# Causal scores packed in 64-key halves: 18 score units a segment in place of 20, with a padded copy of V and a new timetable

## The chip, the cores and the metric

The kernel runs on one core of one Trainium2 chip. The metric is the device time of one execution in microseconds (us). Engines: PE (TensorE), ACT (ScalarE), DVE (VectorE), POOL (GpSimd), SP (SyncE, which here only issues DMAs).

## The reference

The input x has 2048 tokens of 640 features. It is normalized per token, and two blocks read the result xn: block A, attention with 32 heads of 20 features in 4 segments of 512 tokens with a running memory, and block B, a gated MLP of width 1536.

```python
xn = _layernorm(x)
# block A, for each of the 4 segments s (L = 512), all 32 heads:
logits = einsum('bhqd,bhkd->bhqk', qs, ks) * 20**-0.5 + causal_mask
a_dot = einsum('bhqk,bhkd->bhqd', softmax(logits), vs)
a_mem = einsum(phi(qs), M) / (einsum(phi(qs), z) + 1e-6)   # M, z: sums over earlier segments
o = g * a_mem + (1 - g) * a_dot                            # g = sigmoid(beta), per head
M = M + einsum(phi(ks), vs); z = z + sum(phi(ks))
s = o @ wo
# block B and the end
h = (sigmoid(xn @ w_gate) * (xn @ w_up)) @ w_down
out = x + s * silu(h)
```

The mask is causal inside a segment: a query sees the keys up to its own place. phi(t) is t + 1 where t > 0, else exp(t).

## The kernel before

**Scores and attention.** The 32 heads are 8 groups g of 4 heads r. Queries and keys are kept transposed (QT, KT): head r of a group has its 20 features and 3 rows of a softmax bound in partitions 32r to 32r+22, so that the four heads' score matmuls (23 rows by 128 keys) run in four row groups of PE. Their products go to the four PSUM banks of Sps, head r to bank r, keys on the partitions, queries along the bank. One filling of Sps (512 columns in each bank) is a score unit: scores (L544) computes it, exps (L552) makes one exponential of 128x2048 on ACT into a tile pt (4 buffers), and POOL masks the 128 columns at the diagonal of each key block with affine_select (L557).

Of key block kb (128 keys) the queries from 128 kb on are computed: 512, 384, 256 and 128 columns, 1280 a group. pair_units (L44) packs two groups in five units of 512 columns, so a segment has 20 units and the kernel 80.

attend_T (L561) multiplies a group's pt tiles by V. V (Vflat, two buffers, one for each parity of the segment) has tokens on its partitions and for each key block and head 20 features and a column of ones. For each of the four key blocks it issues four matmuls, one per head, side by side in four column groups of 32, all into the bank ApsT: 16 matmuls. Three steps in "turn" (L578 to L594) transpose the result on DVE, divide it (on POOL mostly) and transpose it back. The last group of the last segment goes through attend (L598) and finalize instead, with queries on the output's partitions: 40 matmuls of 21 columns.

**Dense work.** Gate, up and down projections are generators that give one matmul a step (do_gate, do_up, do_down). mm (L117) issues a matmul whole, or as four in column groups of 32 while ORDER["columns"] is set; that is so in a slot that is followed by an attend. PSUM has 4 banks for Sps and 4 (pool ps_d, L96) for all else.

**The order** is written out by hand. Each score unit opens a slot. A slot does the attend that is due in it (visits), then scores and exps of its unit, then events, sorted by their times in the table TIMES (in slots from the segment's start), with dense steps in between so that the work done keeps up with a constant rate per slot (L922 to L948). Events are the projections K, Q and V of the next segment with their evacuations (K_eng, Q_eng, V_eng: a for ACT, v for DVE), layer norm, phi, the memory's parts, spills of Q and K to DRAM and their read-back in the head layout (spill, relayout), the spill of the attention's output (dot_spill) and its read-back in another layout (out_load), and the output projection. After the last unit, the remaining down projections and the output of the last segment follow (tail_*). All DMAs after the start-up are issued by SP in order, except two of the last stores; each waits there until its data are ready.

At the start PE runs a warm-up on a zeroed tile (keep_warm_columns, L636, called at L642), and segment 0 is normalized and projected in straight order (L643 to L754).

Of the kernel before, what the change touches and what calls it, by code (L numbers as in the profile page):

```python
# [43 lines left out]
def pair_units(g):  # L44
    return [[(g, 0, 0, 512, 0)],
            [(g, 1, 0, 384, 128), (g, 3, 384, 128, 384)],
            [(g, 2, 0, 256, 256), (g + 1, 2, 256, 256, 256)],
            [(g + 1, 0, 0, 512, 0)],
            [(g + 1, 1, 0, 384, 128), (g + 1, 3, 384, 128, 384)]]

def segment_units(n):
    units = []
    for g in range(0, NG, 2):
        units += pair_units(g)
    return units

TIMES = dict(
    turn=(0.03, 0.27, 1.29), turn_last=(0.0, 0.135, 0.43), attend=0.36, last=(0.36, 0.75), rest=350, dot6=0.43, load6=0.48,
    dot7=1.92, load7=1.95, add=(4.27, 4.52), out=(5.25, 5.95, 7.25, 8.35, 8.74, 9.06, 9.45, 11.05), update=-1.2,
    mem=(2.23, 4.32, 3.0, 6.98, 6.98, 2.45, 9.09, 10.79), mem_spill=11.56, mem_T=14.4, mem_T_last=12.63,  # L60
    k_tok=2.04, dot3=13.22, dot5=17.84, load5=18.1, add5=19.86, dot6_last=19.55, load6_last=19.6, stats0=(0.53, 0.9, 1.65, 3.6),
    stats=(-0.55, 0.13, 1.32, 3.57), norm=(5.26, 5.72, 6.03, 6.29), norm_T=7.22, ready=12.0,
    K=(9.69, 10.07, 10.49, 13.82, 14.29), Q=(11.32, 11.72, 12.29, 12.45, 13.52), K_eng='vaava', Q_eng='avvav',
    V=(10.33, 13.33, 14.43, 14.63, 17.05, 17.66, 19.78, 20.06), V_eng='avaavvav', k_spill0=14.77, k_lay0=15.15,
    q_spill0=14.1, q_lay0=16.79, q_spill1=15.26, k_spill1=16.93, q_abs=(13.53, 14.84), bound=14.78,
    bound_mm=15.9, bound_lay0=18.6, load_x=13.95, phi_k=((7.15, 7.62, 8.3), (12.77, 13.52, 13.77)),
    phi_q=((16.0, 16.6, 17.12), (18.3, 18.7, 19.18)),
# [8 lines left out]
def kernel(  # L76
# [37 lines left out]

    xt_of, xnT_of = {}, {}
# [29 lines left out]
    warm = stg.tile([P, 3 * L], BF, name="mn")  # L145
    nc.vector.memset(warm[:, 0:L], 0.0)
# [33 lines left out]
    V = [t[:, 0:VN].rearrange("p (j h e) -> p j h e", j=4, e=E1) for t in Vflat]  # L180

# [56 lines left out]
    def ln_norm(n, j, mv, rs):  # L238
        if n > 0 and j < 2:
            if j == 0:  # L240
                seg["xn"] = stg.tile([P, 3 * L], BF, name="mn")
            xn = seg["xn"][:, j * D:(j + 1) * D]
        else:
            xn = lnp.tile([P, D], BF, name="xn", bufs=2)[:]
# [81 lines left out]
    def bound_mm(n):  # L326
# [6 lines left out]
        cb = stg.tile([3 * H, L], BF, name="cb")  # L333
# [23 lines left out]
    def phi_min(n, key, c0, c1):  # L357
        src = seg[n][key][:, c0:c1, :]
        mn = stg.tile([P, 3 * L], BF, name="mn")
# [17 lines left out]
    def m_update(n):  # L377
# [13 lines left out]
        dmb = stg.tile([P, DC, WIN], BF, name="dmb")  # L391
# [111 lines left out]
    HALF = P // 2  # L503
    o6 = cpool.tile([HALF, L], BF, name="o6")
    nc.gpsimd.memset(o6[:].bitcast(mybir.dt.uint32), 0)

    def tail_load():
        src = OTd[(NSEG - 1) % 2]
        nc.sync.dma_start(seg[NSEG - 1]["oT"][R5 - C3:P, 3, :], src[R5:C4, :])
        nc.sync.dma_start(o6[0:R6 - C4, :], src[C4:R6, :])  # L510
# [10 lines left out]
    def tail_add4(j0, j1):  # L521
        t = slice(j0 * P, j1 * P)
        nc.vector.tensor_tensor(seg[NSEG - 1]["oT"][0:HALF, DC - 1, t],
                                tail_po[j0][:].rearrange("p j t -> p (j t)")[0:HALF, :], o6[:, t], op=ALU.add)
# [18 lines left out]

    def scores(unit):  # L544
        for (g, kb, c0, ncol, q0) in unit:
            for r in range(4):
                nc.tensor.matmul(Sps[:, r, c0:c0 + ncol],  # L547
                                 lhsT=KT[32 * r:32 * r + DH + 3, g, kb * P:(kb + 1) * P],
                                 rhs=QT[32 * r:32 * r + DH + 3, g, q0:L],
                                 start=True, stop=True, tile_position=(32 * r, 0))  # L550

    def exps(unit):  # L552
        ntot = sum(u[3] for u in unit)
        pt = ptp.tile([P, 4, L], BF, name="pt")
        nc.scalar.activation(pt[:, :, 0:ntot], Sps[:, :, 0:ntot], ACT.Exp, scale=SCALE)  # L555
        for (g, kb, c0, ncol, q0) in unit:
            nc.gpsimd.affine_select(out=pt[:, :, c0:c0 + P], in_=pt[:, :, c0:c0 + P], compare_op=ALU.is_ge,  # L557
                                    fill=0.0, base=0, pattern=[[0, 4], [1, P]], channel_multiplier=-1)
        return pt

    def attend_T(n, g, todo):  # L561
# [6 lines left out]
        for i, ((_, kb, c0, ncol, q0), t) in enumerate(todo):  # L568
            for r in range(4):
                off = (kb * H + 4 * g + r) * E1  # L570
                nc.tensor.matmul(ps[32 * r:32 * r + 32, q0:L], lhsT=Vflat[n % 2][:, off:off + 32],  # L571
                                 rhs=t[:, r, c0:c0 + ncol], start=(i == 0), stop=(i == len(todo) - 1),
# [25 lines left out]
    def attend(n, todo):  # L598

        if not acc:  # L600
            acc["ps"] = ps_d.tile([P, 4, 4, E1], F32, name="Aps", tag="d")
            acc["blocks"] = 0
        for (g, kb, c0, ncol, q0), t in todo:
            for r in range(4):
                for qb in range(kb, 4):
                    off = c0 + (qb - kb) * P
                    nc.tensor.matmul(acc["ps"][:, qb, r, :], lhsT=t[:, r, off:off + P],
                                     rhs=V[n % 2][:, kb, 4 * g + r, :],
                                     start=(acc["blocks"] == 0 and r == 0 and qb == kb), stop=True,
                                     skip_group_check=True)  # L610
            acc["blocks"] += 1
        if acc["blocks"] == 4:
# [29 lines left out]
    keep_warm_columns(17, L // 2)  # L642
# [17 lines left out]
    def norm0(j, *pieces):  # L660
        nc.vector.reciprocal(rs[:, j:j + 1], rs[:, j:j + 1])
        xns[j] = lnp.tile([P, D], BF, name="xn", bufs=2)
# [79 lines left out]
    bound_dma(0, 0)  # L742
    load_x(1)
# [31 lines left out]
    units = [(n, unit) for n in range(NSEG) for unit in segment_units(n)]  # L775
    units.append((NSEG - 1, None))
    SLOTS, SEG = len(units), 20
    LAST = (NSEG - 1) * SEG
    OLD = LAST + 15
# [7 lines left out]
    for p in range(0, OLD, 5):  # L787
        n, g = units[p][0], units[p][1][0][0]
        visits[p + 4] = (n, g, (p, p + 1, p + 2))
        visits[p + 6] = (n, g + 1, (p + 3, p + 2, p + 4))  # L790
    visits[OLD + 4] = (NSEG - 1, NG - 2, (OLD, OLD + 1, OLD + 2))

# [9 lines left out]
    for slot, (n, g, _) in visits.items():  # L802
        for k in range(3):
            late = g == NG - 1 or slot == OLD + 4
            at(slot + TIMES["turn_last" if late else "turn"][k], 0, turn, n, g, k)

    def last_attend(slots):
        todo = [(p, pts[u]) for u in slots for p in units[u][1] if p[0] == NG - 1]
        attend(NSEG - 1, todo)

    for slot in range(OLD + 1, OLD + 4):
        at(slot + TIMES["attend"], RESERVE, lambda: None)
    at(OLD + 4 + TIMES["last"][0], 500, last_attend, (OLD + 2, OLD + 3))
    at(OLD + 5 + TIMES["last"][1], 500, last_attend, (OLD + 4,))

# [13 lines left out]
    for n in range(NSEG):  # L829
# [7 lines left out]
        if n >= 1:  # L837
# [14 lines left out]
        if n == NSEG - 1:  # L852
            on("dot5", 0, dot_spill, (n, 4, 6))
# [68 lines left out]
    for slot, (n, unit) in enumerate(units):  # L922
        if slot in visits:
            m, g, us = visits[slot]
            attend_T(m, g, [(q, pts[u]) for u in us for q in units[u][1] if q[0] == g])
# [79 lines left out]
```

## Time and profile before

| | |
|---|---|
| three runs, us | 316.82, 316.96 (median), 317.26 |
| the profiled execution, us | 316.93 |
| its span, first to last instruction, us | 315.2 |
| first and last score unit start, us | 35.52 and 296.88 |
| last matmul starts, us | 311.2 |
| ACT: 80 exponentials, us each | 1.878 |
| POOL: 128 masks of 128x512, us each | 0.658 |
| DVE / POOL busy | 72% / 42% |
| DMA, mean | 131 GB/s |

Times inside the span count from its start. An engine's share is busy time over the span; it is an average over stages. In a list of groups, a line gives the source line, engine, operation, tiles, shapes, count, then busy us and mean ns of one, then the engine's idle time just before such instructions and what ended it. The chain that ended last follows the end of the program back to what released each step. L numbers are lines of the kernel before.

### The profile page before, as it was taken

To read this page: it belongs to the slowest core of one execution; us is meant where nothing else is said; L and a number is where in the kernel's file an instruction comes from. 1 tells how busy PE (TensorE), PEld (TensorE's weight loads), DVE (VectorE), ACT (ScalarE), POOL (GpSimd) and SP (SyncE) were. 2 spreads that over 40 slices of the span, in tenths; PEclk is the share of its full clock that TensorE was granted. 3 is DMA by queue.
4 is the path that set the end of the run, shared out by engine and by line. 5 is a ranking of instruction groups with operands and counts; after the bars stand their busy time and mean duration, and the time that the engine had idled before them with its cause. 6 is when DMAs were issued, how large, how long until landed. Compare 5 with 4: busy or idle time off the path is not lost.

```text
span 315.2 us, 10264 instructions
## 1 busy us (share of the span) xinstructions
PE 309.9 (98%) x4329; PEld 167.5 (53%) x4329; DVE 225.7 (72%) x512; ACT 226.8 (72%) x231; POOL 131.6 (42%) x227
## 2 busy tenths in 40 slices
PE   7999999999999999999999999999999999999995
PEld 5544445665545445654665454544466655444673
DVE  6574455665868988878879989788777776644575
ACT  3723478778798776778897869679897775777730
POOL 2680035535262435435453354444434353525313
PEclk9999999999999999999999999999999999999999
DMA  8984886510841364405954445139534000280202
GB/s 250 361 340 144 282 228 163 153 32 2 217 146 65 101 131 148 107 23 150 247 170 123 115 108 152 61 111 215 163 91 125 19 23 30 79 156 16 86 21 85
DMA packets 55247, 41.27 MB, mean 131 GB/s; under 512 B 25953, under 2 KB 53825, under 8 KB 55201
## 3 DMA queue, kind: packets, MB, share of 16 engines
q1 hardware_dynamic: 52656, 35.87, 41.0%
q10 hardware_dynamic: 2544, 4.75, 4.0%
q8 instruction: 34, 0.56, 0.7%
q14 instruction: 13, 0.10, 0.1%
HBM read 19.98 MB, written 14.73 MB: 110 GB/s over the span
## 4 chain that ended last, share of the span: by engine, by line
PE 96%; DVE 2%; DMA 1%; issue 0%
PE up L121 12%; PE yp L121 11%; PE gp L121 11%; PE psq L121 10%; PE Sps L547 8%; PE gp L125 6%; PE yp L125 6%; PE up L125 6%; PE ApsT L571 6%; PE psv L121 5%; PE psq L125 4%; PE sp L121 3%; PE sp L125 3%; PE psv L125 2%; PE sp L531 2%; PE am L121 1%
## 5 line engine op out<-in xcount | busy, mean ns | idle before, releaser
L555 ACT ACTIVATE pt<-Sps 128x2048 bf16<-128x2048 f32 x80 | 150.2, 1878 | 40.9 <-PE Sps L547 39.6
L557 POOL TENSOR_SCALAR_AFFINE_SELECT pt<-pt 128x512 bf16<-128x512 bf16 x128 | 82.2, 658 | 156.2 <-ACT pt L555 153.4
L434 DVE SCALAR_TENSOR_TENSOR hT<-tg,up 128x512 bf16<-128x512 bf16 x48 | 32.5, 678 | 24.0 <-PE up L121 9.7
L121 PE MATMUL up<-xnT,Wu 128*128 128x512 bf16 x159 | 42.5, 380 | 0.0
L121 PE MATMUL gp<-xnT,Wg 128*128 128x512 bf16 x152 | 40.1, 380 | 0.0
L423 ACT ACTIVATE tg<-gp 128x512 bf16<-128x512 f32 x48 | 28.5, 595 | 14.4 <-PE gp L121 10.5
L121 PE MATMUL yp<-Wd,hT 128*128 128x320 bf16 x246 | 38.2, 300 | 0.0
L547 PE MATMUL Sps<-QT,KT 23*128 23x384 bf16 (+3 forms) x512 | 31.9, 301 | 0.0
L121 PEld LDWEIGHTS <-hT 128*128 128x128 bf16 x246 | 22.7, 98 | 11.3 <-issue 3.0
L579 DVE STREAM_TRANSPOSE tb<-ApsT 128x512 f32<-128x512 f32 x31 | 22.0, 711 | 4.2 <-PE ApsT L571 4.0
L451 DVE SCALAR_TENSOR_TENSOR aa<-t,yp 128x320 bf16<-128x320 bf16 x32 | 15.3, 477 | 12.9 <-ACT t L450 12.7
L125 PE MATMUL gp<-xnT,Wg 128*32 128x512 bf16 x352 | 24.4, 380 | 0.0
L571 PE MATMUL ApsT<-pt,V 128*32 128x512 bf16 (+2 forms) x496 | 23.5, 299 | 0.0
L121 PEld LDWEIGHTS <-Wu 128*128 128x128 bf16 x159 | 14.2, 98 | 17.4 <-issue 4.0
L121 PEld LDWEIGHTS <-Wg 128*128 128x128 bf16 x152 | 14.1, 98 | 15.8 <-issue 1.9
L125 PE MATMUL yp<-Wd,hT 128*32 128x320 bf16 x552 | 21.9, 300 | 0.0
L125 PE MATMUL up<-xnT,Wu 128*32 128x512 bf16 x324 | 21.7, 380 | 0.0
L547 PEld LDWEIGHTS <-KT 23*128 23x128 bf16 x512 | 9.1, 92 | 23.4 <-issue 23.4
L591 DVE STREAM_TRANSPOSE obT<-ob 128x256 f32<-128x256 f32 x31 | 13.4, 434 | 11.1 <-POOL ob L588 11.0
L588 POOL TENSOR_TENSOR ob<-tb,rb 128x320 bf16<-128x320 f32 x27 | 19.8, 735 | 2.2
L121 PE MATMUL psq<-xnT,Wq 128*128 128x512 bf16 x85 | 19.5, 379 | 0.0
L571 PEld LDWEIGHTS <-V 128*32 128x32 bf16 x496 | 14.4, 97 | 8.1 <-ACT tg L423 0.2
(124 smaller groups left out, 447.3 us busy)
## 6 DMA issues: line engine op xcount, KB each, us to landing
KT<-Kd SPq DMA_DIRECT2D x32, 80.0 KB
QT<-Qd SPq DMA_DIRECT2D x32, 80.0 KB
out_dram<-xt SPq DMA_DIRECT2D x14, 160.0 KB
Wg<-in_B_w_gate_dram ACTq DMA_DIRECT2D x1, 1920.0 KB
Wu<-in_B_w_up_dram ACTq DMA_DIRECT2D x1, 1920.0 KB
xt<-in_A_x_dram SPq DMA_DIRECT2D x3, 640.0 KB
Wd<-in_B_w_down_dram SPq DMA_DIRECT2D x1, 1920.0 KB
Od<-odot SPq DMA_DIRECT2D x3, 640.0 KB
```

The costliest lines, as they stand in the source:

```text
L121: nc.tensor.matmul(out_, lhsT=lhsT, rhs=rhs, start=start, stop=stop, skip_group_check=True)
L125: nc.tensor.matmul(out_[cols], lhsT=lhsT[:, cols], rhs=rhs, start=start, stop=stop, tile_position=(0, 32 * r), skip_group_check=True)
L423: nc.scalar.activation(tg[:], gp[:], ACT.Tanh, scale=0.5)
L434: nc.vector.scalar_tensor_tensor(out=h[:], in0=seg[n]["tg"][:], scalar=1.0, in1=up[:], op0=ALU.add, op1=ALU.mult)
L451: nc.vector.scalar_tensor_tensor(out=s["aa"][j][:, hs], in0=t2[:], scalar=1.0, in1=yp[:], op0=ALU.add, op1=ALU.mult)
L547: nc.tensor.matmul(Sps[:, r, c0:c0 + ncol], lhsT=KT[32 * r:32 * r + DH + 3, g, kb * P:(kb + 1) * P], rhs=QT[32 * r:32 * r + DH + 3, g, q0: ...
L555: nc.scalar.activation(pt[:, :, 0:ntot], Sps[:, :, 0:ntot], ACT.Exp, scale=SCALE)
L557: nc.gpsimd.affine_select(out=pt[:, :, c0:c0 + P], in_=pt[:, :, c0:c0 + P], compare_op=ALU.is_ge, fill=0.0, base=0, pattern=[[0, 4], [1, P ...
L571: nc.tensor.matmul(ps[32 * r:32 * r + 32, q0:L], lhsT=Vflat[n % 2][:, off:off + 32], rhs=t[:, r, c0:c0 + ncol], start=(i == 0), stop=(i == ...
L579: nc.vector.transpose(tb[:].rearrange("p h e -> p (h e)"), ps[:].rearrange("p (a t b) -> p a b t", t=32, b=2))
L588: eng.tensor_tensor(to, of, by, op=ALU.mult)
L591: nc.vector.transpose(s["obT", g // 4][:, g % 4, :].bitcast(F32), ob[:].rearrange("p a e b -> p (a e b)").bitcast(F32))
```

## The change

The causal triangle is cut finer, in blocks of 64 keys, and the pieces are packed anew. The units of four groups (e to e+3) are nine, in the order A, B, Y, A, W, A, Y, A, B; a segment has 18 and the kernel 72. All are full, 512 columns in each bank.

- A: key block 0. Keys 0-63 give partitions 0-63 and queries 0-511; keys 64-127 give partitions 64-127 and queries 64-511. The 64 columns left over in the upper half take keys 128-191 with queries 128-191.
- B: key block 1 from query 192, and key block 2 from query 320, both with all 128 keys.
- W: key block 2 from query 320 and key block 3 from query 448, for two groups, all 128 keys.
- Y: key block 1 from query 192 (two halves of 64 keys), key block 3 from query 448 of a group (two halves), and the two 64x64 triangles at keys 256 and 384 for two groups, one in each half.

A and Y issue their matmuls with 64 keys (23 rows by 64 columns of the array); A has 12 matmuls, B 8, W 16 and Y 32. The number of score matmuls goes from 512 to 1152.

The 64x64 triangles at queries 0, 128, 256 and 384 need V of 64 keys only; for them there is a padded copy Z, whose other 64 partitions are zero. Z holds the 16 heads of half a segment. fill_Z copies V into it with two DMAs on SP, once in the start-up and then twice a segment (slots 1.97 and 10.49). An attend has 8 pieces in place of 4, five of 64 columns, 32 matmuls. attend for the last group cuts queries in 64: 80 matmuls.

POOL masks 64 columns per diagonal block: A takes two affine_selects, B two, W two, Y four.

All times of the table are new. Seven of eight V evacuations per segment are on ACT (four before), four of five of K (three before), and two of Q as before. The read-back of the first 512 rows of a segment's attention output (load6) is at 0.58 of the next segment, the fill of Z at 1.97, and the spill and read-back of the rest (dot7, load7) at 2.29 and 2.54. Small tiles share a buffer (tag sc: xn of the fourth token block, cb, dmb, o6), xn of the first three is in mn, and the warm-up has 38 rounds of 112 columns in place of 17 of 256.

```diff
+    for e in range(0, NG, GH):
+        units += [("A", e), ("B", e), ("Y", e + 1), ("A", e + 1), ("W", e + 1),
+                  ("A", e + 2), ("Y", e + 2), ("A", e + 3), ("B", e + 3)]
...
+    ZW = H // 2 * E1
+    Zflat = cpool.tile([P, 4 * ZW + 32 - E1], BF, name="Z")
+    Z = Zflat[:, 0:4 * ZW].rearrange("p (a b w) -> p a b w", a=2, b=2)
+
+    def fill_Z(n, h):
+        src = Vflat[n % 2][0:HALF, 0:VN].rearrange("p (a b k w) -> p a b k w", a=2, b=2, k=2)
+        for b in range(2):
+            nc.sync.dma_start(Z[HALF * b:HALF * b + HALF, :, b, :], src[:, :, b, h, :])
...
+        nc.gpsimd.memset(Zflat[:], 0.0)
...
+    def products(pieces):
+        for out_, keys, g, q0, q1 in pieces:
+            m, p0 = keys.stop - keys.start, out_[0]
+            for r in range(4):
+                rows = slice(32 * r, 32 * r + DH + 3)
+                nc.tensor.matmul(Sps[p0:p0 + m, r, out_[1]:out_[1] + q1 - q0], lhsT=KT[rows, g, keys],
+                                 rhs=QT[rows, g, q0:q1], start=True, stop=True, tile_position=(32 * r, p0))
+
+    def early(c0, g):
+        return [((0, c0), slice(256, 320), g, 256, 320), ((HALF, c0), slice(384, 448), g, 384, 448)]
+
+    def halves(c0, g, k0, q0, q1):
+        return [((0, c0), slice(k0, k0 + HALF), g, q0, q1), ((HALF, c0), slice(k0 + HALF, k0 + P), g, q0, q1)]
+
     def scores(unit):
-        for (g, kb, c0, ncol, q0) in unit:
-            for r in range(4):
-                nc.tensor.matmul(Sps[:, r, c0:c0 + ncol],
-                                 lhsT=KT[32 * r:32 * r + DH + 3, g, kb * P:(kb + 1) * P],
-                                 rhs=QT[32 * r:32 * r + DH + 3, g, q0:L],
-                                 start=True, stop=True, tile_position=(32 * r, 0))
+        kind, g = unit
+        k = slice
+        if kind == "A":
+            products([((0, 0), k(0, 64), g, 0, L), ((HALF, 64), k(64, 128), g, 64, L),
+                      ((HALF, 0), k(128, 192), g, 128, 192)])
+        elif kind == "B":
+            products([((0, 0), k(128, 256), g, 192, L), ((0, 320), k(256, 384), g, 320, L)])
+        elif kind == "W":
+            products([((0, 0), k(256, 384), g, 320, L), ((0, 256), k(256, 384), g + 1, 320, L),
+                      ((0, 192), k(384, 512), g, 448, L), ((0, 448), k(384, 512), g + 1, 448, L)])
+        else:
+            e, end = (g - 1, g - 1) if g % GH == 1 else (g, g + 1)
+            products(halves(0, g, 128, 192, L) + halves(320, end, 384, 448, L) + early(384, e) + early(448, e + 1))
...
-    def attend_T(n, g, todo):
+    def attend_T(n, g):
...
+        todo = pieces(n, g, "ABYW")
+        for i, (values, v, t, c0, q0, q1) in enumerate(todo):
             for r in range(4):
-                off = (kb * H + 4 * g + r) * E1
-                nc.tensor.matmul(ps[32 * r:32 * r + 32, q0:L], lhsT=Vflat[n % 2][:, off:off + 32],
-                                 rhs=t[:, r, c0:c0 + ncol], start=(i == 0), stop=(i == len(todo) - 1),
+                src, off = values(v, r)
+                nc.tensor.matmul(ps[32 * r:32 * r + 32, q0:q1], lhsT=src[:, off:off + 32],
+                                 rhs=t[:, r, c0:c0 + q1 - q0], start=(i == 0), stop=(i == len(todo) - 1),
                                  tile_position=(0, 32 * r), skip_group_check=True)
...
-    keep_warm_columns(17, L // 2)
+    keep_warm_columns(38, 112)
...
     bound_dma(0, 0)
+    fill_Z(0, 0)
     load_x(1)
...
+        for h in range(2):
+            if n or h:
+                at(t0 + TIMES["fill"][h], 0, fill_Z, n, h)
```

In pieces (new), a group's eight pieces are listed as unit, V's key block or Z's, first column in pt, and queries:

```python
out = [(a, 0, 64, 64, L), (a, "Z0", 0, 0, 64), (a, "Z1", 0, 128, 192),
       (b, 1, 0, 192, L), (c, 2, c2, 320, L),
       (y, "Z2", z, 256, 320), (y, "Z3", z, 384, 448), (d, 3, c3, 448, L)]
```

An attend reads units of slots at least two before its own, as it did (the last group's aside).

More of the change, by code (lines that the diff above doesn't have):

```diff
@@ L55, in segment_units @@
     return units
 TIMES = dict(
[L58 to L66, printed above, removed]
@@ L552, in exps @@
     def exps(unit):
-        ntot = sum(u[3] for u in unit)
+        kind, g = unit
         pt = ptp.tile([P, 4, L], BF, name="pt")
[L555 to L558, printed above, removed]
-        return pt
-    def attend_T(n, g, todo):
+        nc.scalar.activation(pt[:], Sps[:], ACT.Exp, scale=SCALE)
@@ L596, with attend @@
     acc = {}
-    def attend(n, todo):
+    def attend(n, which):
         if not acc:
             acc["ps"] = ps_d.tile([P, 4, 4, E1], F32, name="Aps", tag="d")
-            acc["blocks"] = 0
-        for (g, kb, c0, ncol, q0), t in todo:
+            acc["begun"] = set()
+        for values, v, t, c0, q0, q1 in pieces(n, NG - 1, which):
             for r in range(4):
[L605 to L609, printed above, removed]
+                src, off = values(v, r)
+                for q in range(q0, q1, HALF):
+                    p0 = q % P
+                    nc.tensor.matmul(acc["ps"][p0:p0 + HALF, q // P, r, :],
+                                     lhsT=t[:, r, c0 + q - q0:c0 + q - q0 + HALF], rhs=src[:, off:off + E1],
+                                     start=p0 not in acc["begun"], stop=True, tile_position=(0, p0),
                                      skip_group_check=True)
-            acc["blocks"] += 1
-        if acc["blocks"] == 4:
+                    acc["begun"].add(p0)
+        if "B" in which:
             finalize(n, NG - 1, 0, 4)
@@ L775 @@
     units = [(n, unit) for n in range(NSEG) for unit in segment_units(n)]
+    unit_of = {(n, *unit): slot for slot, (n, unit) in enumerate(units)}
     units.append((NSEG - 1, None))
-    SLOTS, SEG = len(units), 20
+    SLOTS, SEG = len(units), 4 * GH + 2
     LAST = (NSEG - 1) * SEG
-    OLD = LAST + 15
+    OLD = LAST + SEG // 2
     events = []
@@ L786 @@
     visits = {}
[L787 to L791, printed above, removed]
+    for n in range(NSEG):
+        for g in range(NG if n < NSEG - 1 else NG - 1):
+            visits[unit_of[n, "A", g - g % GH] + 4 + 2 * (g % GH)] = (n, g)
+    LATE = unit_of[NSEG - 1, "Y", NG - 2] + 2
     def out_item(n, i):
@@ L800, in turn @@
         seg[n]["turn", g][k]()
-    for slot, (n, g, _) in visits.items():
+    for slot, (n, g) in visits.items():
         for k in range(3):
-            late = g == NG - 1 or slot == OLD + 4
+            late = g == NG - 1 or slot == LATE
             at(slot + TIMES["turn_last" if late else "turn"][k], 0, turn, n, g, k)
[L807 to L811, printed above, removed]
+    for slot in range(LATE - 3, LATE):
         at(slot + TIMES["attend"], RESERVE, lambda: None)
-    at(OLD + 4 + TIMES["last"][0], 500, last_attend, (OLD + 2, OLD + 3))
-    at(OLD + 5 + TIMES["last"][1], 500, last_attend, (OLD + 4,))
+    at(LATE + TIMES["last"][0], 500, attend, NSEG - 1, "AY")
+    at(LATE + 1 + TIMES["last"][1], 500, attend, NSEG - 1, "B")
     st = {}
@@ L923 @@
         if slot in visits:
-            m, g, us = visits[slot]
-            attend_T(m, g, [(q, pts[u]) for u in us for q in units[u][1] if q[0] == g])
+            attend_T(*visits[slot])
             done += AV_NS
```

86 lines of the change are left out of this document (62 added, 24 removed).

## The prediction

> **What bounds the kernel now.** I read the page first: busy shares, then the chain that ended last, then the waits of PE alone.
>
> ```profile
> span 315.2 us, 10264 instructions
> ...
> PE 309.9 (98%) x4329; PEld 167.5 (53%) x4329; DVE 225.7 (72%) x512; ACT 226.8 (72%) x231; POOL 131.6 (42%) x227
> ...
> PE 96%; DVE 2%; DMA 1%; issue 0%
> ...
> L555 ACT ACTIVATE pt<-Sps 128x2048 bf16<-128x2048 f32 x80 | 150.2, 1878 | 40.9 <-PE Sps L547 39.6
> ```
>
> The waits of PE, over the whole span:
>
> ```profile
> PE wps L639 <- DVE mn L146: 1.2, 1, 1.2
> PE pT L674 <- DVE xn L664: 0.2, 1, 0.2
> PE psv L121 <- ACT xnT L679: 0.2, 1, 0.2
> ```
>
> All 1.6 us of them lie in the start-up. From then on PE runs one unbroken stream, and ACT, with the largest single group, waits 39.6 us for PE's scores. So time is what the PE stream costs. A saving on ACT, DVE or POOL is worth nothing by itself, and a new wait of PE costs its full length. The granted clock is 9 in all slices of the page, so nothing is to be had there.
>
> The price of each kind of PE work comes from the chain, which lists PE's pieces end to end (start, us, what), here two stretches of it:
>
> ```profile
> 91.60 0.65 PE up L121 x3
> 92.25 0.33 PE Sps L547 x8
> 92.58 0.32 PE up L121
> ...
> 95.55 0.33 PE Sps L547 x4
> 95.88 1.19 PE up L125 x20
> 97.07 0.86 PE gp L125 x16
> 97.94 0.64 PE dm L387 x79
> ...
> 99.02 0.54 PE ApsT L571 x16
> ```
>
> ```profile
> 298.07 0.59 PE Aps L607 x24
> 298.66 3.00 PE yp L121 x22
> 301.66 0.39 PE Aps L607 x16
> ```
>
> Read from it: a dense 512-column matmul is 0.65/3 = 0.217 us, that is 0.416 ns a column (the matmul forms agree: scores of 512 and 384 columns last 384 and 332 ns, 52 ns for 128 columns). A score unit is 512 columns in each of four row groups at once, 0.213 us of streaming, yet it takes 0.33, with one set of four matmuls (x4) or two (x8), and the first dense matmul after it takes 0.32 instead of 0.217 (0.11 more; 1.19 instead of 1.08 for x20). So a unit costs 0.33 + 0.11 = 0.44 us, half of it for changing the shape of the array and back. An attend is 0.54 us for 1280 columns (0.533). The 63-column matmuls of L387, four column groups side by side, step by 0.64/79 = 8.1 ns, 32 ns for a set of four. The last group's 21-column matmuls take 0.59/24 = 24.5 ns.
>
> **The change, part by part.** Times are against the profiled execution, 316.93 us (span 315.2 and 1.7 around it), 0.03 under the median 316.96. Dense matmuls (gate, up, down, K, Q, V, output) keep their columns; more of them go in the four-column-group form, which costs the same (1.08 against 1.08 for five matmuls of 512).
>
> 1. Fewer score units: 80 units cost 80 x 0.44 = 34.8 us (0.435 unrounded). After: 32 A, 16 B, 8 W, 16 Y. The wide pieces of B and W are of the known kind: B 0.435, W with two more sets 0.445. In A and Y two halves of 64 keys write PSUM partitions 0-63 and 64-127. No row of before shows row groups and column groups split at once. The nearest are L547 (four row groups at once) and L125/L571 (four column groups at once, each with its own moving data), and both are fully parallel, so I take the halves as parallel. The second half of A begins up to 4 x 8.1 = 0.03 us late; I take 0.02: A 0.455. Y streams 320 columns (0.133) and then three pairs of 64-column sets, at 0.032 a pair by the L387 row or 0.065 if the eight matmuls step by 8.1: 0.133 + 0.096 in place of 0.213, plus 0.02, gives 0.47 (0.57 at the far end). Sum 32 x 0.455 + 16 x 0.435 + 8 x 0.445 + 16 x 0.47 = 32.6: **-2.2 us** (-3.2 without the late start, -0.6 with the far Y). The halves in series are a rival below.
>
> 2. Attend: 31 groups, still 1280 columns, but 8 sets instead of 4, five of 64 columns. At 32 ns instead of 26.7 each, five add 0.029, times 31 is +0.9; at streaming price 0. In L387 eighty loads come one behind another, here short sets stand between sets of 448, 320 and 192 columns that cover their loads, so I take the middle, **+0.45**.
>
> 3. The last group's attend: 40 matmuls of 24.5 ns become 80 of 64 by 21 in two halves of the array. Bounds 8.1 (four column groups) and 24.5 each: 0.65 to 1.96 against 0.98; two halves, 16 ns, 1.3: +0.3. It stood among dense matmuls of its own shape; now it changes shape twice a call, two calls, 4 x 0.11 = 0.44. **+0.75** (0.1 to 1.4).
>
> 4. ACT: eight exponentials fewer, 8 x 1.878 = 15 us; in the timetable three V evacuations (0.44) and one K (0.58) per segment go from DVE to ACT, 5.7 us in all. Off the path: ACT already waits for PE. Nothing.
>
> 5. POOL: 128 masks of 512 elements become 176. The row gives 0.64 for 512 elements, the Mbd selects (L203, 168 elements) 0.40; 256 lies near 0.46. A 1.1, B 0.9, W 1.3, Y 2.2 us a unit: 97 us against 82. It is hidden because the nearest use is two slots later (7 us; a slot is now (296.88 - 35.52)/79 = 3.3 us and becomes some 3.7), while scores, exponential and Y's four masks need 0.3 + 1.9 + 2.2 = 4.4. Without that cover PE would wait in the attend.
>
> 6. The padded V: two issues per fill, eight fills, all on SP. The nearest row (four of L340 in 1.35 us) gives 0.35 an issue, 0.7 a fill. A fill waits on the attend that last read Z; behind it on SP stand the spill and read-back of the last eighth of the output, k_tok, or the spill of the memory part. The read-back of the first 512 rows of the output, which waits for its spill (L476 waits 2.5 us at most), is issued at slot 0.58, ahead of the fill at 1.97, so the fill can't start before it; the first reader is at slot 4, 7 us after. The second fill (10.49, reader 13) has 9 us. Nothing; a fill later than its reader costs its lateness. The fill ahead of the x load, the Wd load and the second spills in the start-up pushes these 0.7 us, against a first down-projection at 53.9 us. The zeroing of Z on POOL (about 1.2 us, by the 0.8 us of 840 elements at L199) delays constants that are first used far later.
>
> 7. Start-up and tail: warm-up 38 x 112 columns against 17 x 256, nearly the same sum; buffers shared (sc, mn) have users tens of us apart. Nothing; bounds ±0.3.
>
> Sum: -2.2 + 0.45 + 0.75 = -1.0: **315.9 us**. Ends of the terms: -3.1 to +1.7, so 313.8 to 318.6.
>
> **The rivals.** (a) *The halves run in series* (the other side). If a second half in the same row group waits for the first, A and Y stream 1024 columns: 48 x 0.213 = 10.2 us more, 326 us. It decides from 1.0/10.2, a tenth of the overlap lost. For it: no row shows this shape. Against: four column groups, with all rows in common, do run side by side, and weight loads of L387 go out every 8 ns while matmuls last 196. [...]
>
> (b) *ACT's queue holds PSUM.* The twelve evacuations that move to ACT can stand behind an exponential: 1.88 + 0.44 = 2.3 us, while PE has three other banks of its four to fill, 3 x 0.68 = 2.0 us with V pieces. Each one caught so stops PE 0.3 us: 12 x 0.3 = 3.6, 319.5 us. For it: PE now has no slack at all. Against: 20 of 32 V evacuations are on ACT already and not one stops PE, and eight exponentials go. It decides when ACT runs over 2 us behind.
>
> (c) *No real change*: the small sets and the last group eat the gain (Y at 0.57, attend +0.9), 317 to 318; this is the upper part of my own case.
>
> **How the numbers follow.** The forecast's case (halves parallel, no new wait) 0.72, from 313.8 to 318.6; a measurement here tells 0.2% (0.6 us) from no change, and of the 0.72, 0.44 lies under 316.3, 0.18 within, 0.10 over 317.6, since the middle is -1.0 and the high end as near as the low. Series 0.10, ACT's queue 0.15 (spread 318 to 321), another wait 0.03: all slower. Faster 0.44, same 0.18, slower 0.38. The range 314.2 to 320.0 leaves out the outer ends of the first case, the upper part of (b), and (a).
>
> **What the profile after would show.** Right: waits of PE still under 2 us; in the chain an A unit of 0.35 and a Y unit under 0.4, next dense piece 0.11 longer; attends 0.54 to 0.57; ACT's wait for scores longer; POOL near 146 us. Wrong: A units of 0.55 (series); PE waiting on ACT V or on POOL pt, or on DMA Z; dense pieces longer than 1.08.

## The result, and the profile after

| | before | after |
|---|---|---|
| median, us (6 runs each) | 317.12 (316.82 to 317.30) | 321.49 (319.90 to 322.21) |
| ratio, 95% interval | | 1.0132 (1.0118 to 1.0146) |
| profiled execution, its span, us | 316.93, 315.2 | 322.21, 320.5 |
| first K matmul starts, us | 13.19 | 14.14 |
| last matmul starts, us | 311.22 | 316.50 |

The changed kernel is 1.3% slower. The forecast was 315.9 with a range to 320.0; the median lies above it. The page of the changed kernel (instructions, PE's busy time, the shares of the chain, the two groups around the scores, the instruction queue):

```profile
span 320.5 us, 13555 instructions
...
PE 311.1 (97%) x5928; PEld 182.7 (57%) x5928; DVE 217.8 (68%) x500; ACT 217.7 (68%) x235; POOL 144.9 (45%) x276
...
q8 instruction: 46, 0.75, 1.0%
...
PE 94%; DMA 2%; issue 1%; ACT 1%; DVE 1%; SPq 0%; ACTq 0%
...
L589 ACT ACTIVATE pt<-Sps 128x2048 bf16<-128x2048 f32 x72 | 135.2, 1878 | 48.2 <-PE Sps L560 47.0
L592 POOL TENSOR_SCALAR_AFFINE_SELECT pt<-pt 128x256 bf16<-128x256 bf16 (+3 forms) x176 | 93.4, 544 | 141.8 <-ACT pt L589 138.6
...
L560 PE MATMUL Sps<-QT,KT 23*64 23x64 bf16 (+6 forms) x1152 | 30.3, 260 | 3.1 <-issue 2.9
```

ACT is further off the path than before: it waits 47.0 us for scores (39.6 before). What is new stands at the end of the last line: PE was idle 3.1 us ahead of a score matmul, and 2.9 of them are "issue", so PE waited for nothing that the semaphores show. The five longest waits of PE say it once more, and name a DMA in the start-up:

```profile
PE Sps L560 <- issue: 2.9, 1, 2.9
PE wps L711 <- DVE ktok L145: 1.2, 1, 1.2
PE psv L120 <- DMA Wv<-in_A_wv_dram: 0.5, 1, 0.5
PE wps L706 <- DVE rs L733: 0.4, 1, 0.4
PE Sps L560 <- ACT pt L589: 0.2, 1, 0.2
```

**The work of PE went as forecast.** Two stretches of the chain after (start, us, what):

```profile
88.43 0.35 PE Sps L560 x8
88.79 0.76 PE up L124 x12
...
91.73 0.55 PE ApsT L642 x24
92.28 0.36 PE Sps L560 x32
92.65 0.54 PE gp L120 x2
...
99.14 0.55 PE ApsT L642 x32
99.69 0.33 PE Sps L560 x8
```

```profile
301.96 1.04 PE Aps L679 x48
...
306.37 0.73 PE Aps L679 x32
```

An A unit takes 0.35 us and a Y unit 0.36 (32 matmuls), against 0.33 of a whole unit. Half a unit in the upper partitions therefore runs beside the lower half, and so do 64-column sets. An attend takes 0.55, as against 0.54. The last group's two calls take 1.04 + 0.73 = 1.77 us (0.98 before), and the dense matmul ahead of each call takes 0.23 instead of 0.136.

**Where the 5.28 us went** (last matmul, 316.50 less 311.22). First the stop, in the timeline of PE (start, us, engine, line, tiles, count, idle before):

```profile
157.83 0.20 PE L642 MATMUL ApsT<-pt,V 128*32 128x64 bf16 x4
157.97 0.39 PE L560 MATMUL Sps<-QT,KT 23*64 23x320 bf16 x20
161.28 0.25 PE L560 MATMUL Sps<-QT,KT 23*64 23x64 bf16 x12 [2.92 <-issue]
161.47 4.43 PE L120 MATMUL yp<-Wd,hT 128*128 128x320 bf16 x19
```

PE stops in the middle of a Y unit, between two matmuls of one loop, both of 64 columns, with 12 of its 32 still to come. Nothing in the program stands between them. The start of a matmul to the next is 3.11 us there, 3.08 more than elsewhere. The table by stretch (us, busy time of PE, PEld, DVE, ACT, POOL, then granted clock, DMA share, GB/s) shows what lies ahead of it and behind it:

```profile
154.00:158.00 4.00, 4.00 (x133) 3.02 (x134) 2.54 (x6) 4.00 (x6) 3.67 (x6) 1.00 0.88 261
158.00:161.30 3.30, 0.38 (x33) 0.26 (x27) 1.76 (x3) 0.46 (x2) 0.00 (x0) 1.00 0.49 155
161.80:165.20 3.40, 3.40 (x15) 1.90 (x14) 0.79 (x3) 2.09 (x2) 1.45 (x4) 0.50 0.67 209
```

Ahead of the stop the transfer engines are almost full (0.88); behind it the granted clock is 0.50 for 3.4 us. In these 3.4 us twelve 320-column matmuls take 0.267 us instead of 0.136, and one at the border 0.218: 12 x 0.131 + 0.08 = 1.65 us more. What the transfer engines carry is in SP's timeline:

```profile
147.90 0.39 SPq L311 DMA_DIRECT2D Qd<-qtd  x1
148.39 4.43 SPq L472 DMA_TRANSPOSE oTm<-Od  x1
152.87 0.58 SPq L131 DMA_DIRECT2D xt<-in_A_x_dram  x1
153.50 0.49 SPq L311 DMA_DIRECT2D Kd<-ktd  x1
154.10 0.42 SPq L311 DMA_DIRECT2D Qd<-qtd  x1
```

The queue "instruction" gives the likely cause. Its packets of 16,384 bytes come while the program runs, 46 of them for the 11,878 PE instructions in the trace, 34 for 8,691 before: one for 256 to 258 instructions. So a packet seems to bring a block of PE's program, and each comes about when PE enters the block before it; the border of a block is taken here where the promptest packets start, 160 to 170 instructions past each multiple of 256. PE entered a block at 153.93 and had used it up at 158.00, in 4.07 us. The packet of the next started at 158.77, when the burst was over, 4.84 us after the entry; it landed at 159.81, and PE went on at 161.28. In the trace of before the same burst put a packet off by 3.71 us (to 153.07), but that block lasted 8.88 us, and PE did not stop.

Second, the start-up. In the changed kernel the rows of Wv and K read

```profile
8.72 1.52 PE L120 MATMUL psv<-Wv,xnT 128*128 128x320 bf16 x10 [0.52 <-DMA Wv<-in_A_wv_dram]
...
14.14 5.56 PE L120 MATMUL psq<-xnT,Wk 128*128 128x512 bf16 x25
```

and in the kernel before

```profile
7.59 1.52 PE L121 MATMUL psv<-Wv,xnT 128*128 128x320 bf16 x10
...
13.19 5.56 PE L121 MATMUL psq<-xnT,Wk 128*128 128x512 bf16 x25
```

K starts 0.95 us later: DVE waits 0.68 for the second x block (its first came 0.27 earlier than before), PE 0.52 for Wv. The account: start-up 0.95, stop 3.08, slow clock 1.65, one wait on an exponential 0.25, together 5.93; so what is left for the work of PE is 5.28 - 5.93 = -0.65.

### The profile page after: what moved, and what is told of

It is laid out like the page before. It is cut to its first block, busy times and chain, and to the rows that moved or that the text cites. A ratio compares the mean times of both kernels' runs of the same rounds, so it can differ in the third digit from the quotient of the medians.

```text
span 320.5 us, 13555 instructions
## 1 busy us (share of the span) xinstructions
PE 311.1 (97%) x5928; PEld 182.7 (57%) x5928; DVE 217.8 (68%) x500; ACT 217.7 (68%) x235; POOL 144.9 (45%) x276
## 4 chain that ended last, share of the span: by engine, by line
PE 94%; DMA 2%; issue 1%; ACT 1%; DVE 1%; SPq 0%; ACTq 0%
PE up L120 11%; PE gp L120 10%; PE psq L120 10%; PE yp L120 9%; PE yp L124 8%; PE Sps L560 8%; PE gp L124 6%; PE up L124 6%; PE ApsT L642 5%; PE psq L124 4%; PE psv L124 3%; PE sp L124 3%; PE psv L120 3%; DMA Wv<-in_A_wv_dram 2%; PE sp L120 2%; PE sp L542 1%
## 5 line engine op out<-in xcount | busy, mean ns | idle before, releaser
L589 ACT ACTIVATE pt<-Sps 128x2048 bf16<-128x2048 f32 x72 | 135.2, 1878 | 48.2 <-PE Sps L560 47.0
L592 POOL TENSOR_SCALAR_AFFINE_SELECT pt<-pt 128x256 bf16<-128x256 bf16 (+3 forms) x176 | 93.4, 544 | 141.8 <-ACT pt L589 138.6
L560 PE MATMUL Sps<-QT,KT 23*64 23x64 bf16 (+6 forms) x1152 | 30.3, 260 | 3.1 <-issue 2.9
L120 PE MATMUL yp<-Wd,hT 128*128 128x320 bf16 x200 | 32.4, 311 | 0.0
L124 PE MATMUL yp<-Wd,hT 128*32 128x320 bf16 x736 | 28.5, 300 | 0.0
L560 PEld LDWEIGHTS <-KT 23*64 23x64 bf16 (+1 forms) x1152 | 14.5, 101 | 19.6 <-issue 17.7
L124 PE MATMUL up<-xnT,Wu 128*32 128x512 bf16 x356 | 25.2, 380 | 0.0
L124 PEld LDWEIGHTS <-hT 128*32 128x32 bf16 x736 | 19.4, 97 | 6.6 <-issue 1.8
L642 PE MATMUL ApsT<-pt,V 128*32 128x448 bf16 (+2 forms) x496 | 23.2, 273 | 0.0
L458 ACT ACTIVATE t<-yp 128x320 bf16<-128x320 f32 x32 | 13.9, 436 | 11.8 <-PE yp L120 7.3
```

Of the source, the lines that this page charges most:

```text
L120: nc.tensor.matmul(out_, lhsT=lhsT, rhs=rhs, start=start, stop=stop, skip_group_check=True)
L124: nc.tensor.matmul(out_[cols], lhsT=lhsT[:, cols], rhs=rhs, start=start, stop=stop, tile_position=(0, 32 * r), skip_group_check=True)
L458: nc.scalar.activation(t2[:], yp[:], ACT.Tanh, scale=0.25)
L560: nc.tensor.matmul(Sps[p0:p0 + m, r, out_[1]:out_[1] + q1 - q0], lhsT=KT[rows, g, keys], rhs=QT[rows, g, q0:q1], start=True, stop=True, ti ...
L589: nc.scalar.activation(pt[:], Sps[:], ACT.Exp, scale=SCALE)
L592: nc.gpsimd.affine_select(out=blocks(pt[rows]), in_=blocks(pt[rows]), compare_op=ALU.is_ge, fill=0.0, base=base, pattern=pattern, channel_ ...
```

## The experiments

Theory 1: the new score pieces more than double the score matmuls, PE uses up a block of its program faster than the next arrives in a burst of transfers, stops, and loses the clock. Its rivals: the 64-key shapes or an evacuation cost the time wherever they stand; the stop is an accident of one execution. For the start-up several causes were tried in turn. Ratios are against the kernel before, from runs on the same chip. Of the timetable a diff shows only the entries that change, and of a long diff the main lines.

**e1_after_again.** No edit.

> The changed kernel once more, for a second trace of it. Theory 1 (PE ran out of instructions: the page of 256 that it needed was asked for in a DMA burst and came 4.8 us later): PE stops again for 2 to 4 us between 150 and 165 us, inside a unit or an attend and not at a semaphore, right where the 16 KB instruction packet came late; time 319.9 to 322.2. Theory 2 (the stop belongs to the Y unit or to a wait of the new timetable): it stands at the same instruction again, whatever the packets do, or in several Y units. Start-up, theory S1 (the longer warm-up brings the first page fetch into the first loads): the second x block and Wv again land 0.5 us later than before; S2 (chance): they land as in the kernel before.

321.68 us, ratio 1.0125 (1.0055 to 1.0194); the interval is wide, since one of the four runs took 318.12. The stop is in the same Y unit again, 2.15 us, up to 161.79, its packet at 159.6; K starts at 15.58. Behind this shorter stop the clock stayed at 1.0. It was 0.50 in the start-up, from 7.34 to 10.75, behind a wait of 1.75 us in the warm-up, and that is about 1.0 us of this late start (from the first matmul of V to K 7.96 us, against 6.98 in e2). So stop and late start-up both come again in the kernel, with sizes that vary.

**e2_x_load_early.** The load of the x block leaves the burst.

```diff
-    load_x=13.03
+    load_x=10.6
```

> The changed kernel with one time changed: the x load of the segment after next (640 KB) at slot 10.6 in place of 13.03, so that it no longer runs behind the transposing read-back of the memory part, in the burst of 149 to 158 us. Theory 1: the instruction page is late by less than its page lasts (4 us), the stop of 3 us is gone or under 1 us, and with it the lower clock after it: 317 to 318.5. Theory 2: the stop stays and so does the time, 319.9 to 322.2.

319.63, ratio 1.0078 (1.0063 to 1.0093), so 2.05 us under e1 and clear of the 1.0118 to 1.0146 of the result, but above the 318.5 that was expected. The stop at 158 us is gone: SP issues the x load at 145.69 instead of behind the transposes, and the next packets come at 152.0 and 157.1. Part of the gain went to new waits of PE, among them

```profile
PE psq L120 <- DMA xnT<-Xd: 0.8, 1, 0.8
...
PE yp L120 <- issue: 0.6, 1, 0.6
```

The wait for the transposes of xnT (0.8) need not come from the moved load: e3 leaves the load where it was, and has this wait too (1.0). The second wait without a semaphore ends at 62.37 us, 1.45 us after an instruction packet landed, that is, it looks like another late block.

**e3_old_warmup.** The warm-up of the kernel before.

```diff
-    keep_warm_columns(38, 112)
+    keep_warm_columns(17, L // 2)
```

> The changed kernel with the warm-up of before (17 rounds of 256 columns, 168 PE instructions fewer, none of them later than 5 us). S1: the first instruction page is fetched later than 6.1 us, the first dense matmul starts near 6.2 us as before in place of 6.7, and the second at 7.6 in place of 8.7: 1 us less, and by the shift of all page borders the late page may fall elsewhere. S2: start-up as in the run beside it, time the same within 0.5 us.

320.08, ratio 1.0107 (1.0074 to 1.0140). The first instruction packet moves from 6.1 to 12.2 us, out of the start-up loads, and the x block is as late as ever (K at 14.02). A fetch among the start-up loads is not what delays them. The stop near 158 us is gone here: 84 matmuls fewer shift every block's border behind them. So the Y unit by itself does not stop PE; where a border falls matters.

**e4_before_all_in_columns.** The kernel before, all dense matmuls in four column groups: 6615 matmuls instead of 4329, with the old scores.

```diff
-        ORDER["columns"] = slot + 1 in visits
+        ORDER["columns"] = True
```

> The kernel before with all dense matmuls of the main loop issued as four in column groups (2286 matmuls and as many weight loads more, same columns, same price per five matmuls in the chain, fewer shape changes none). Theory 1: pages of 256 instructions run out in 3 to 6 us, and PE stops for instructions in the DMA bursts, several times: 2 to 10 us more, 319 to 327, with PE waits that name no semaphore. Theory 2: no stop, 316.5 to 317.5.

319.08, ratio 1.0068 (1.0053 to 1.0083). The wait without a semaphore appears in the kernel before as well, with none of the new shapes:

```profile
PE Sps L547 <- issue: 0.5, 1, 0.5
```

It is one, which ends at 166.91, 1.5 us after a packet landed; from start to start it is 0.81 us, 0.65 more than in other such units. Theory 1 had expected several. Of the 2.0 us of longer span, 0.65 are this stop and 0.37 another wait, at 104.10; the cause of the rest, about 0.9, was not found. A larger program alone makes few stops. Its start-up is not late (K at 13.15), although its program is larger than the changed kernel's.

**e5_fewer_in_burst.** The changed kernel with fewer PE instructions around the burst: whole matmuls in three slots.

```diff
-        ORDER["columns"] = slot + 1 in visits
+        ORDER["columns"] = slot + 1 in visits and slot not in (30, 32, 34)
```

> The changed kernel with the dense matmuls of three slots of segment 1 (30, 32 and 34 of 72, around 145 to 162 us) issued whole and not in column groups: some 250 PE instructions fewer just there, 0.2 us more for changes of shape per slot, no DMA moved. Theory 1 (the page of instructions comes late in the DMA burst): the page lasts longer than its fetch is late, the stop of 2 to 3 us at 158 us is gone or under 1 us, and so is the lower clock behind it; 317.5 to 319.5. If DMA order were the cause without the number of instructions: stop stays, 320 to 322. Start-up is not touched: K begins at 14 us or later as in the three runs of the changed kernel, if its cause is in the kernel; at 13.2 in some of them, if it is chance.

319.39, ratio 1.0071 (1.0050 to 1.0092). The transfers stay where they were, PE's dense work is the same, and the trace has no stop at 158 us and no drop of the clock; K starts at 14.38. The block that PE enters at 147.9 now lasts 10.3 us, over nearly the whole burst, and the next packet starts at 159.18, only 1.0 us after the next entry. So with e2 both sides are tried: the stop goes when the transfers move, and when the instructions there become fewer.

**e6_xT_and_x_early.** e2, and the transposes of xnT earlier too.

```diff
-    norm_T=6.96, load_x=13.03
+    norm_T=6.2, load_x=10.6
```

> The changed kernel with two DMA times moved ahead: the x load at slot 10.6 (as in the run before) and the transposing read-back of the normalized x at 6.2 in place of 6.96, 2.7 us earlier. Theory: the stop at 158 us stays away, and the 0.8 to 1.0 us that PE waited for that read-back near 70 us goes as well: 318.3 to 319 where the first alone had 319.6; what is left over before is the start-up.

318.20 (10 runs), ratio 1.0036 (1.0021 to 1.0051). No wait of PE behind the start-up is longer than 0.25 us. The start-up is 1.6 us later than in before (K at 14.80). From the first K matmul to the last matmul it takes 297.73 us, with 0.4 of waits in it (0.25 on the exponential, 0.13 where the stop was); the kernel before takes 298.03. So the work of PE is 0.7 less, as in the account of the result. Two edits of the timetable give back some 3 of the 4.4 us.

**e7_before_x_late_ktok.** The kernel before, with the x load put into its burst and the warm-up reading ktok, as in the changed kernel.

```diff
-    load_x=13.95
+    load_x=14.45
-    warm = stg.tile([P, 3 * L], BF, name="mn")
+    warm = stg.tile([P, 4, D], BF, name="ktok")[:, 0, 0:L]
```

> The kernel before with the DMA order of the changed one in the burst (x load behind the read-back of the memory part, slot 14.45 for 13.95) and the warm-up reading the changed kernel's tile (ktok). Theory 1: no stop, since its pages last 8 to 9 us there: 316.8 to 317.4. If the DMA order alone were the cause, PE would stop here too: 319 and more. Start-up: if the warm-up's tile delays the loads, K begins 0.8 us later than 13.2, else not.

317.70, ratio 1.0020 (1.0008 to 1.0033), above the 317.4 of theory 1 and far from the 319 of its rival; in its trace no stop, and K at 13.15. The burst alone does not stop the old program. The tile of the warm-up alone does not make the start-up late.

**e8_pad_aligned, e9_before_misaligned, e10_aligned_and_early.** Z is 1686 bytes larger than the tile whose place it takes, and so the tiles behind it begin at other addresses modulo 256. e8 puts them back in the changed kernel, e9 puts them off in the kernel before, e10 is e8 with the edits of e6.

```diff
+    pad = cpool.tile([P, 48], BF, name="pad")
```

> The changed kernel with an unused tile of 96 bytes a partition among the constants, so that the x block and every tile behind it begin again at the addresses modulo 256 bytes that they have in the kernel before (x block at 0 instead of 160). Theory A, addresses: the loads of the start-up and the transposes run at the speed of before; the first K matmul starts at 13.1 to 13.4 us instead of 14.0 to 15.6, and the median falls by 0.8 to 1.6 us, to 319.9 to 320.9, more if the stop in the slot at 158 us goes as well (318). Rival B, the addresses do not matter and the late start-up comes from something else that the larger program brings: the first K matmul stays at 14.0 to 15.6 us and the median at 321.2 to 321.9.

> The kernel before with an unused tile of 160 bytes a partition among the constants: the x block then begins at 160 modulo 256 bytes, as in the changed kernel, and nothing else is changed. Theory A, addresses: the first K matmul moves from 13.2 to 14.0 us or later, and the median from 317.1 to 317.9 to 318.7. Rival B: the first K matmul stays at 13.2 us and the median at 316.9 to 317.4.

> The changed kernel with the 96-byte tile, the load of the next x block at 10.6 instead of 13.03 of a slot pair's clock and its transposes at 6.2 instead of 6.96. Theory A, addresses, with the two earlier edits worth the 3.5 us that they gave together (318.2): start-up at 13.2 us, no stop of PE longer than 0.3 us, and 316.4 to 317.2, so level with the kernel before (317.1) or better by up to 0.7, about the saving in PE's work. Rival B: 318 to 318.5, as without the tile.

e8 321.9, ratio 1.0147 (1.0110 to 1.0183), K at 14.49; e9 317.11, ratio 1.0000 (0.9991 to 1.0008), K at 13.24. Addresses are not the cause. e8's stop is 2.80 us, and the clock falls to 0.5 for 3.4 us behind it. e10: 317.83, ratio 1.0033 (1.0018 to 1.0048), K at 14.48, with e6 the best of the changed kernels and still behind before. Its waits of PE, behind that at the start of the warm-up:

```profile
PE psv L120 <- DMA Wv<-in_A_wv_dram: 1.1, 1, 1.1
PE Sps L562 <- issue: 0.5, 1, 0.5
PE Sps L562 <- ACT pt L591: 0.2, 1, 0.2
```

The "issue" is the old stop, between the same two matmuls of the same Y unit, now 0.62 us, though the x load is out of the burst: the packet started 2.48 us after the entry into a block of 4.07 us, and even so PE stopped.

**e11_no_fill, e12_before_copies.** The changed kernel without the copies into Z, and the kernel before with as many copies added.

```diff
-        nc.gpsimd.memset(Zflat[:], 0.0)
+        nc.gpsimd.memset(Zflat[:], 1.0)
...
-    fill_Z(0, 0)
...
-                at(t0 + TIMES["fill"][h], 0, fill_Z, n, h)
```

> The changed kernel without the 16 transfers that copy values into the padded V (its places stay at 1, so the attention of this kernel is not the reference's). It leaves out 2048 packets of 84 bytes and up on SP's queue, the first of them at 32 us, and nothing else. Theory A, the whole set of transfers that a program holds changes how its first loads run: the first K matmul starts at 13.1 to 13.4 us and the median falls by 0.9 to 1.6 us, to 320.0 to 320.8, by more if the stop near 158 us goes as well. Rival B, the copies only cost what they move, at 32 us and later: the first K matmul stays at 14.0 to 15.6 us and the median within 0.5 of 321.5. Under both, the copies are shown to be free (within 0.5) or not once the start-up is set aside.

> The kernel before with a 160-byte unused tile among the constants and 16 transfers that copy parts of V into it, 2048 packets in all, at the times of a slot pair at which the changed kernel fills its padded V. Theory A: the first K matmul moves from 13.2 to 14.0 us or later and the median from 317.1 to 318.0 to 318.8. Rival B: 13.2 us, and the median 317.0 to 317.5.

e11 322.82, ratio 1.0175 (1.0142 to 1.0209), above what either theory allowed, K at 14.26, a stop of 2.45 us with the clock at 0.5 behind it. It has two more waits of PE, 1.9 us on a gate activation; their cause is not known. e12 317.22, ratio 1.0003 (0.9994 to 1.0013), K at 13.77 in its one trace. In the kernel before the copies cost nothing, and in the changed one taking them out does not cure the start-up. A late first K matmul, in e12, did not need the new scores.

**e13_weights_later, e14_before_weights_later.** e6 and the kernel before, with Wk and Wq loaded 2 to 4 us later and from ACT, so that they do not share the engines with x and Wv. Wg and Wu follow further back.

```diff
-    load_w(nc.sync, Wk, A_wk)
-    load_w(nc.sync, Wq, A_wq)
...
-    load_w(nc.scalar, Wg, B_w_gate)
+    load_w(nc.scalar, Wk, A_wk)
...
-    load_w(nc.scalar, Wu, B_w_up)
+    load_w(nc.scalar, Wq, A_wq)
```

> The changed kernel with the load of the next x block at 10.6 and its transposes at 6.2 (the pair of edits that gave 318.2), and in the start-up the loads of Wk and Wq issued from ACT where Wg and Wu were, Wg and Wu behind the third and the sixth V part. Theory A, the 1.6 MB of Wk and Wq, issued at 2.7 to 4.2 us on SP, share the transfer engines with the second x block and Wv and delay them: no wait for x or Wv behind the first x block, the first K matmul at or before 13.2 us instead of 14.8, and 316.4 to 317.2 in all. Rival B, the first 0.5 MB arrive late by themselves: K at 14 us or later, 317.8 to 318.6.

> The kernel before with the same move of the four weight loads in the start-up. Theory A: its start-up had 0.15 to 0.2 us of such waits at most, so the first K matmul moves from 13.2 to 12.9 to 13.2 us and the time stays at 316.8 to 317.2; the runs of 317.4 and above, which this kernel also shows, become fewer. Rival B: 317.1 as before, with the same spread of 316.9 to 317.6.

e13 319.15, ratio 1.0062 (1.0040 to 1.0084), K at 14.10; e14 317.98, ratio 1.0016 (1.0003 to 1.0030), K at 13.23. Both medians lie above what either theory allowed. The wait for Wv stays in e13, and a wait for the transposes is back:

```profile
PE psq L120 <- DMA xnT<-Xd: 1.2, 1, 1.2
...
PE psv L120 <- DMA Wv<-in_A_wv_dram: 0.6, 1, 0.6
```

The first half megabyte is late without these loads beside it. The kernel before loses by this edit, with a new wait of 0.7 us up to 25.89.

## Why the prediction was wrong

Direction and range were both wrong. Point by point:

1. *Score units, -2.2*: right in mechanism. From the starts of the matmuls, with the changes of shape on both sides, A is 0.458, B 0.434, W 0.439, Y 0.471, each within 0.01 of its term; together 32.6 us, as forecast, against 34.6 before (34.8 in the working): -1.9.
2. *Attend, +0.45*: 0.55 against 0.54 in the chain, 31 x 0.01 = +0.3. In its range.
3. *Last group, +0.75*: +1.0, in its range, but the parts are off both ways. The matmuls take 22 ns each where 16 was taken (+0.79 for +0.3), and the changes of shape 0.19 where 0.44 was taken. That the sum is near is luck.
4. *ACT, nothing*: one wait of 0.25 us on an exponential, none on an evacuation. Right within that.
5. *POOL, 97 us, hidden*: 93.4 us (the forecast's own prices add up to 95), and PE never waited for a mask.
6. *The copies, nothing*: right in time. One issue took 0.60 us, not the 0.35 of the row I took, but no wait of PE came of it, and e12 is at 1.0003.
7. *Start-up, nothing, bounds 0.3*: wrong, +0.95 in the profiled execution and +0.8 to +2.4 in the traces of the changed kernel and its variants (about 1.0 of the 2.4 is e1's slow clock).

Steps 1 to 3 give -0.6 by the pieces; the stream as a whole gives -0.65 in the profiled execution and -0.7 in e6, where -1.0 was forecast. **The step that failed is the sentence that the time is "what the PE stream costs", with the 0.03 left for "another wait"**: the sum priced each matmul by its columns and shape, and took it for granted that the instructions are there and that the clock stays at full. The change adds 640 score matmuls, 496 of attends, 40 of the last group and 84 of the warm-up; with more of the dense work in four column groups it is 1599 in all, each with its weight load: 4329 to 5928. Fewer columns were bought with a third more instructions. In the trace of before the risk could be read: the instruction queue stands on the page (34 packets), one of its packets was 3.71 us late in the burst, and the block before it lasted 8.88. The forecast used neither. The stop with its clock is 3.08 + 1.65 = 4.7 of the 5.3 us.

The rivals: the halves in series (326) are refuted by 0.35 and 0.36 us: here halves of the same row group, in different column groups, overlap. ACT's queue (319.5) would have shown waits on V; there are none. "No real change" had the right work of PE, nearly, and missed the rest.

Of the mechanism behind the stop, shown by experiment is that it needs both sides: it goes when the x load leaves the burst (e2, e6; 0.62 us are left in e10) and when the instructions become fewer there (e5), and is not there when the borders of the blocks are shifted (e3). That the late packet is a block of PE's program is read from its number, size and time. The place agrees: in the result, e8, e10 and e11 PE stops after the same 5569 instructions in the trace, 193 past a multiple of 256, and in e4, another program, 188 past one. The sizes agree too. "Left" is the time from the start of the packet to the end of the block in hand, which lasts 4.07 us in each of these traces (its end is counted as 24 recorded instructions ahead of the place of the stop):

| | packet starts after the entry, us | left, us | stop, us |
|---|---|---|---|
| after | 4.84 | -0.77 | 3.08 |
| e8 | 4.80 | -0.73 | 2.80 |
| e11 | 4.30 | -0.23 | 2.45 |
| e1 | 4.18 | -0.12 | 2.15 |
| e10 | 2.48 | 1.59 | 0.62 |
| e6 | 2.00 | 2.07 | 0.13 |
| e2 | 1.10 | 2.96 | none |

Stop and time left add up to 2.0 to 2.3 us in the first six, and in e2 more than that was left. So a packet that is late by less than its block lasts can still stop PE. No run changed the fetch itself.

**What stays open** is the late start-up. In all ten profiles of the changed kernel and its variants K starts at 14.0 to 15.6 us; in five of the six of the kernel before and its variants at 13.15 to 13.24, in e12 at 13.77. The late bytes are those of 2.5 to 4 us: the packets of x take up to 0.86 us there, against 0.39 before. Taking away the long warm-up (e3), the shifted addresses (e8), the copies (e11) or the loads beside x and Wv (e13) does not cure it, and the warm-up's tile (e7), a larger program (e4) or shifted addresses (e9) alone do not bring it into the kernel before. Each of these rests on one trace, and e12 shows that the kernel before, with copies added, can start late too.

## What to carry to other kernels

When PE is the bound and never waits, count its instructions as well as its columns: read from the trace how many of them a 16,384-byte instruction packet brings, how long they last PE in the densest stretch, and how late such a packet comes in the longest burst of transfers. They have to last longer than the packet is late, here by 2.0 to 2.3 us. Where they do not, move a large load out of the burst, or use whole instead of split matmuls there, before cutting shapes finer. A saving of 1 us is easily lost to a single stop, which may cost half again in clock behind it (here 3.08 us and 1.65).

## What the runs showed of the hardware

- Matmuls of 23 rows by 64 columns in the same row group, one for the lower and one for the upper 64 output partitions, ran side by side: a unit of 12 of them took 0.35 us, against 0.33 with whole key blocks.
- A stop of PE of 2.45, 2.80 or 3.08 us (e11, e8, after) was followed by 3.4 us at a granted clock of 0.50; one of 2.15 us (e1) was not.
- The changes of the clock lie whole multiples of 3.4133 us apart: in the result 157.01 = 46 x 3.4133 and 153.60 = 45 x 3.4133. With stretches of that length, cut at these changes, what fits all 16 traces is how busy PE was in a stretch. Behind the 21 stretches with PE busy for 1.49 us or less the clock was 0.50, among them 0.51 (after), 1.18 (e11), 1.46 (e8) and 1.49 us (e1, start-up); behind the 1444 with 1.65 us or more it was full. e1's stop fell into two stretches, busy for 2.28 and 2.55 us.
- PE went on 1.2 to 1.5 us after the late instruction packet landed: 1.47 (after), 1.21 (e1), 1.45 (e2, at 62.37), 1.50 (e4), 1.29 (e8), 1.33 (e10), 1.46 us (e11).
